# Attention with a soft mixture of experts: two heads at once on the row halves of TensorE

## The chip, the cores and the metric

The kernel runs on one NeuronCore of a Trainium2 chip. Its engines run side by side, each with its own queue, in the order in which the kernel issues the work: TensorE (PE; the loading of its weights is shown as PEld), VectorE (DVE), ScalarE (ACT), GpSimd (POOL) and SyncE (SP), which issues the DMAs here. The metric is the device time of one execution in microseconds (us); lower is better.

## The reference

For 8 batches of 8 heads, 576 positions and 64 dimensions per head, causal in blocks of 64:

```python
scores = 1/sqrt(D) * q @ k.T
scores = where(block_i >= block_j, scores, -1e9)       # blocks of 64 positions
attn = softmax(scores);  x = attn @ v                  # -> x: (8*576, 512)
logits = x @ phi                                       # (4608, 32): 8 experts x 4 slots
d = softmax over all 4608 rows of logits;  slot_input = d.T @ x
slot_out[e] = relu(slot_input[e] @ w1[e]) @ w2[e]      # 8 experts, 512 -> 1024 -> 512
out = softmax over slots of logits @ slot_out
```

All is float32. The weights w1 and w2 are 32 MB, in 32 pieces of 1 MB.

## The kernel before

The work has two stages. The attention stage handles 64 heads, in 32 pairs. The expert stage follows, from line 641: it turns the accumulated slot inputs into hidden rows (up, line 777), into slot outputs (down, line 804) and into the output (emit, line 739). The change leaves it as it is, except for one buffer count.

A head's 576 query rows are cut into tiles of 128 rows, called blocks 4, 3, 2, 1, from the end of the sequence, and a last 64 rows, block 0, which the two heads of a pair fill up to 128 together. Block t needs 128t + 64 columns of keys, so 576, 448, 320, 192 and 64. The upper 64 rows of a block are one step later in the sequence than the lower 64, so the lower ones have their last 64 columns masked (line 293, a matmul that adds -1e30; line 302 for block 0).

Scores (qk, lines 278 to 302). A float32 product is made out of rounded float32 (fp32r) matmuls over all 128 rows of the array: ACT rounds q (qh, line 204), POOL subtracts (ql, line 246), POOL scales k into the upper or lower 64 rows of ks (line 258), and DVE writes what the rounding lost into the other 64 rows (line 266). The two terms of k lie above each other in the 128 rows, q stands there twice, and two matmuls, with qh and with ql, add up a block of scores. Blocks 4 and 3 have two PSUM banks of their own (s43), blocks 2 and 1 share one (s21), block 0 takes one of three that rotate.

Softmax: DVE takes the negative row maximum (rowmax, line 310), ACT the exponential with the row sum (expo, line 316, followed by a read of the accumulator), DVE the reciprocal (zinv, lines 329 and 330), and DVE (block 3) or POOL (the others) multiplies (norm, lines 336 and 338).

Transposes (tr, lines 342 to 364; tr0, line 376). PE turns each 128 x 128 square of the probabilities in one matmul against an identity, with the probabilities as weights and the identity's 128 columns streaming; squares that are half masked are turned as 64 columns against a swapped identity (line 356), which puts two of them side by side. That is 14 per head and one per pair for block 0, in three banks A, B and C per head; ACT or DVE copies each bank out whole (evac).

Product with v (pv, line 390): the two heads of a pair write the two column halves of the array, in plain fp32, one key chunk of 128 after another. Block 0's queries share the first chunk's bank positions, and the last 64 columns have a product of their own. The transposed result xT is copied out (evac_x).

Mixture work, once per batch (four pairs): logits (part, lines 409 and 417), statistics, transposes of the logits and of xT (natural, xnat, line 497), and the accumulation of slot inputs (slots, line 510). It is spread over the next pairs.

What sets the order: every operation is put on a list with a due time (at); the times are in a table TM, in units of a head's period T, found beforehand by a planner. The list is sorted by time and issued in that order, and each engine and SP's queue keep it. EN says which engine does a copy. The weights are loaded in the attention stage as far as there is room (15 pieces stay resident in the arena, seven more come into areas as these become free), the rest in the expert stage.

Of the kernel before, what the change touches and what calls it, by code (L numbers as in the profile page):

```python
# [17 lines left out]
DM = H * D  # L18
# [9 lines left out]
COFF = {0: 0, 1: 576, 4: 1024, 2: 1088, 3: 1408}  # L28


NXN = 4
NXT = 6
NLK = 2
NV = 1
RINGX = "p4_0"
WARM = 11
RES = 15

PB = {4: 2, 3: 2, 2: 2, 1: 2}
XIN = (2,)  # L40
AREAS, LATE0 = {}, 0
for name, n in (
    ("lq0", S), *((f"lk{i}", S) for i in range(NLK)), ("lq1", S),
    *((f"p{t}_0", 128 * t + 64) for t in (4, 3, 2, 1) if PB[t] == 2 and f"p{t}_0" != RINGX), *((f"v{i}", 640) for i in range(NV - 1)),
    *((f"x{i}", S) for i in XIN), *((f"p{t}_{PB[t] - 1}", 128 * t + 64) for t in (4, 3, 2, 1)), ("pz", 128),
    ("pt0", 1600), ("pt1", 1600), *((f"v{i}", 640) for i in range(NV - 1, NV) if f"v{i}" != RINGX), ("phi", 512),
):
    AREAS[name] = (LATE0, LATE0 + n)
    LATE0 += n
NPIECE = 32  # L50
# [13 lines left out]
    "trC": 7.184, "evB": 10.029, "evA": 10.362, "evC": 7.809, "xb": 7.710, "xa": 2.149, "stats": (0, 12.875),  # L64
    "stats2": (0, 19.703), "nlt": (0, 13.687), "ndt": (0, 28.697), "disp": (0, 31.225), "xn0": (0, 3.906),
# [4 lines left out]
    "nltz": (0, 651.278), "ndtz": (0, 897.612), "dispz": (0, 2265.477), "xn0z": (0, 157.597),  # L70
    "en0z": (0, 396.824), "xn1z": (0, 749.778), "en1z": (0, 829.471), "xn2z": (0, 152.238),
    "en2z": (0, 478.997), "xn3z": (0, 651.280), "en3z": (0, 1377.835), "xn4z": (0, 1321.640),
    "en4z": (0, 2191.828), "saccz": (0, 2345.380), "loadq": 0.763, "loadk": 1.523, "loadv": -3.409,
# [7 lines left out]
}  # L81
EN = {
# [3 lines left out]
}  # L86
NB = B
# [4 lines left out]
def tile_attention_softmoe(  # L92
# [17 lines left out]
    swap = const.tile([128, 128], F32, name="swap")  # L110
    for i in range(2):
        nc.vector.tensor_copy(out=swap[:, 64 * i:64 * i + 64], in_=ident[:, 64 - 64 * i:128 - 64 * i])
# [10 lines left out]
    maskr = const.tile([128, 128], BF16, name="maskr")  # L123

    maskq = const.tile([128, 128], BF16, name="maskq")
    for x in (maskl, maskr, maskq):
        nc.vector.memset(x, 0.0)
    nc.vector.memset(maskq[0:1, 64:128], 1.0)
    for i in range(2):
        own, oth = slice(64 * i, 64 * i + 64), slice(64 - 64 * i, 128 - 64 * i)  # L130
        nc.vector.memset(maskl[32 * i:32 * i + 1, own], 1.0)
        nc.vector.memset(maskr[32 * i:32 * i + 1, oth], NEG)
# [32 lines left out]
    with ExitStack() as c1:  # L165
        xp = c1.enter_context(tc.tile_pool(name="xp", bufs=1, side="right"))
        sm = c1.enter_context(tc.tile_pool(name="sm", bufs=4, side="right"))
        ps = c1.enter_context(tc.tile_pool(name="ps", bufs=1, space=PSUM))
        ps_x = c1.enter_context(tc.tile_pool(name="ps_x", bufs=3, space=PSUM))

        s43 = ps.tile([128, 1024], F32, name="s43")
        s21 = ps.tile([128, 512], F32, name="s21")

# [744 lines left out]
```

## Time and profile before

| | us |
|---|---|
| median of three runs (491.8 to 493.0) | 491.83 |
| the profiled execution, whole | 491.81 |
| its span, first to last instruction | 490.0 |
| granted TensorE clock, mean of the span | 0.974 |

Stages of the profiled execution: scores from 6.4, the last scores at 397.7, the last product with v starts within the group from 405.8 to 409.3, experts from 423.7 to the end. A row of the profile gives line, engine, operation, what is written from what, shape, count, and then busy time in all and mean ns of one, and the idle time of the engine just before, with what ended it. In a timeline the columns are start, length, engine, line and operation, and how many like ones were merged.

### The profile page before, as it was taken

The page shows a single profiled execution, that of the slowest core. Times are in us where ns is not written, and L with a number is a line of the kernel's source. Part 1 is how long each engine was busy: PE and PEld are TensorE (multiplying, and loading weights), DVE is VectorE, ACT ScalarE, POOL GpSimd, SP SyncE. Part 2 cuts the span into 40 slices and gives each one's busy share as a digit, 9 for nine tenths or more (in the row PEclk, how much of TensorE's full clock was granted, in tenths as well). Part 3 has the DMA queues.
Part 4 walks back from the last instruction along what each step waited for, and adds up shares of the span by engine and source line. Part 5 has one row for each costly group of instructions (what it writes and reads, how often), then busy time and mean ns, then how long its engine had stood idle before and what let it go on. Part 6 is the DMA issues. An engine that isn't in the chain of part 4 may idle for free.

```text
span 490.0 us, 11349 instructions
## 1 busy us (share of the span) xinstructions
PE 466.9 (95%) x3815; PEld 310.3 (63%) x3815; DVE 396.5 (81%) x992; ACT 344.3 (70%) x1043; POOL 268.8 (55%) x372
## 2 busy tenths in 40 slices
PE   7899999999999999999999999999999999799990
PEld 3766676667666766676766676667666756344660
DVE  5999988988898889888988898989898973244571
ACT  3788788878787778777877787778777863012660
POOL 6776765666666666665666666656665730101100
PEclk9699999999999999999999999999999999799996
DMA  5735635455353544533654426354332119599698
GB/s 146 226 99 184 194 99 159 118 177 183 99 175 105 176 149 139 173 110 117 164 183 129 149 89 196 115 138 109 110 88 67 47 54 415 212 383 413 203 290 290
DMA packets 42697, 81.73 MB, mean 167 GB/s; under 512 B 8720, under 2 KB 26128, under 8 KB 38544
## 3 DMA queue, kind: packets, MB, share of 16 engines
q1 hardware_dynamic: 42640, 81.02, 52.1%
q8 instruction: 30, 0.49, 0.4%
q14 instruction: 27, 0.22, 0.2%
HBM read 71.57 MB, written 9.44 MB: 165 GB/s over the span
## 4 chain that ended last, share of the span: by engine, by line
PE 90%; DVE 3%; ACT 2%; DMA 1%; issue 1%; SPq 1%; POOL 0%; DVEq 0%; POOLq 0%; ACTq 0%
PE pv L390 23%; PE s L287 22%; PE pt_C L362 6%; PE pt_B L362 4%; PE pt_A L362 4%; PE xn L497 4%; PE pt_B L356 4%; PE hp L777 3%; PE so L804 3%; PE pt_A L356 3%; PE o L739 2%; PE lg L409 2%; PE s L293 2%; PE si L510 2%; PE lg L417 2%; PE s L301 1%
## 5 line engine op out<-in xcount | busy, mean ns | idle before, releaser
L316 ACT ACTIVATE arena<-s,stat 128x320 f32<-128x320 f32 (+4 forms) x256 | 135.7, 538 | 50.9 <-DVE stat L310 41.5
L338 POOL TENSOR_SCALAR arena<-arena,stat 128x320 f32<-128x320 f32 (+2 forms) x192 | 104.1, 554 | 95.5 <-DVE stat L329 88.1
L310 DVE TENSOR_REDUCE stat<-s 128x1 f32<-128x320 f32 (+4 forms) x288 | 136.1, 516 | 14.0 <-PE s L287 13.9
L287 PE MATMUL s<-ks,qh 128*128 128x320 f32 (+4 forms) x320 | 122.9, 384 | 1.6 <-ACT arena L316 1.6
L390 PE MATMUL pv<-arena 128*64 128x512 f32 (+5 forms) x768 | 117.1, 409 | 0.0
L246 POOL TENSOR_TENSOR ql<-arena,qh 128x576 fp32r<-128x576 f32 x64 | 91.5, 1429 | 32.5 <-ACT qh L204 29.9
L287 PE MATMUL s<-ks,ql 128*128 128x320 f32 (+4 forms) x320 | 101.3, 317 | 0.8 <-POOL ql L246 0.8
L287 PEld LDWEIGHTS s<-ks,qh 128*128 128x128 f32 (+1 forms) x320 | 60.2, 188 | 29.9 <-ACT arena L204 13.0
L266 DVE SCALAR_TENSOR_TENSOR ks<-arena,ks 64x576 fp32r<-64x576 f32 x64 | 75.1, 1174 | 4.9 <-POOL ks L258 3.0
L390 PEld LDWEIGHTS pv<-arena 128*64 128x64 f32 (+1 forms) x768 | 41.3, 134 | 51.0 <-issue 40.4
L287 PEld LDWEIGHTS s<-ks,ql 128*128 128x128 f32 (+1 forms) x320 | 58.8, 184 | 1.4 <-POOL ql L246 1.2
L316 ACT ACTIVATION_READ_ACCUMULATOR arena<-s,stat 128x1 f32 x256 | 52.5, 205 | 0.0
L258 POOL TENSOR_SCALAR ks<-arena 64x576 fp32r<-64x576 f32 x64 | 42.7, 667 | 12.4 <-PE s L287 9.0
L204 ACT CAST qh<-arena 128x576 fp32r<-128x576 f32 x64 | 43.4, 678 | 8.6 <-DMA arena<-in_q 5.0
L336 DVE TENSOR_SCALAR arena<-arena,stat 128x448 f32<-128x448 f32 x64 | 43.6, 682 | 0.0
L293 PE MATMUL s<-maskr,maskq 128*128 128x64 bf16 x192 | 39.4, 205 | 0.0
L204 ACT COPY arena<-pt_A 128x512 f32<-128x512 f32 x64 | 38.4, 600 | 0.5 <-PE pt_A L362 0.4
L204 ACT COPY arena<-pt_B 128x512 f32<-128x512 f32 x64 | 37.7, 590 | 0.4 <-PE pt_B L362 0.4
L362 PE MATMUL pt_C<-ident,arena 128*128 128x128 f32 x224 | 35.3, 275 | 0.0
L293 PEld LDWEIGHTS <-maskq 128*128 128x128 bf16 x192 | 18.6, 97 | 21.0 <-issue 14.2
L330 DVE RECIPROCAL stat<-stat 128x2 f32<-128x2 f32 (+1 forms) x160 | 26.5, 166 | 5.5
L362 PE MATMUL pt_A<-ident,arena 128*128 128x128 f32 x160 | 27.9, 273 | 0.0
(166 smaller groups left out, 776.7 us busy)
## 6 DMA issues: line engine op xcount, KB each, us to landing
arena<-in_w SPq DMA_DIRECT2D x30, 1024.0 KB, 7.7
arena<-in_q SPq DMA_DIRECT2D x128, 144.0 KB, 3.0
arena<-in_k SPq DMA_DIRECT2D x32, 288.0 KB, 3.4
arena<-in_v SPq DMA_DIRECT2D x32, 256.0 KB, 3.2
out<-arena SPq DMA_DIRECT2D x16, 512.0 KB, 4.1
wr<-in_w SPq DMA_DIRECT2D x2, 1024.0 KB, 8.4
arena<-in_v SPq DMA_DIRECT2D x32, 32.0 KB, 2.7
out<-arena SPq DMA_DIRECT2D x16, 64.0 KB, 3.2
```

Of the source, the lines that this page charges most:

```text
L204: nc.scalar.copy(out=out, in_=in_)
L246: (nc.gpsimd if EN["ql"] == "g" else nc.vector).tensor_tensor(out=qld, in0=src, in1=qhd.bitcast(F32), op=ALU.subtract)
L258: nc.gpsimd.tensor_scalar(out=ks[own, sl], in0=src, scalar1=SCALE, scalar2=0.0, op0=ALU.mult, op1=ALU.add)
L266: nc.vector.scalar_tensor_tensor(out=ks[oth, sl], in0=src, scalar=SCALE, in1=ks[own, sl].bitcast(F32), op0=ALU.mult, op1=ALU.subtract,)
L287: nc.tensor.matmul(pss[t][0:n, lo:hi], lhsT=qq[:, o:o + n], rhs=ks[:, k0 + lo:k0 + hi], start=(i == 0), stop=(i == 1 and not mask),)
L293: nc.tensor.matmul(pss[t][:, hi - 64:hi], lhsT=maskq, rhs=maskr[:, 64:128], start=False, stop=True)
L310: nc.vector.tensor_reduce(out=st[:, 0, u:u + 1], in_=src, axis=AX.X, op=ALU.max, negate=True)
L316: nc.scalar.activation(out=pr, in_=src, func=AF.Exp, bias=st[:, 0, u:u + 1], accum_out=st[:, 1, u:u + 1])
L336: nc.vector.tensor_scalar(out=pr, in0=pr, scalar1=st[:, 2, u:u + 1], scalar2=None, op0=ALU.mult)
L338: nc.gpsimd.tensor_scalar(out=pr, in0=pr, scalar1=st[:, 2, u:u + 1], scalar2=0.0, op0=ALU.mult, op1=ALU.add)
L362: nc.tensor.transpose(out=ptb[bank][:, o:o + 128], in_=probs[h, t][:, 128 * c:128 * c + 128], identity=ident)
L390: nc.tensor.matmul(xps[m, lo][64 * j:64 * j + 64, 0:n], lhsT=v_of(m)[0:k, j, c, :], rhs=pt_of(2 * m + j)[0:k, o:o + n], start=(c == cs[0]) ...
```

## The change

Both heads of a pair are worked on together, and the array is used in row halves: head 0 in rows 0 to 63, head 1 in rows 64 to 127.

- Scores are plain fp32: q comes as one load of 640 columns for the pair (block 0's rows padded with zeros), k is scaled for both heads in one POOL instruction, and there is no qh, ql or second term of k. qk has three steps per pair: U1 (block 4, first 512 columns), U2 (block 3 and the 64-column tail of block 4), U3 (blocks 2 and 1). In each the two heads' matmuls alternate. One masking matmul per head closes U2 and U3. Block 0 is one plain matmul over the whole array.
- Each head has two PSUM banks (sc): blocks 4 and 3 fill them, and blocks 2 and 1 go into the first of them after block 4 has been read. Two banks (ptb) take all transposes, and two (xbk) everything else, each at a bank given in the table.
- Transposes are of 64 rows by 128 columns against a 64 x 64 identity, upper half into one bank, lower half into the other. A head has two groups: group 1 is key chunks 0 and 1, group 2 chunks 2 to 4; tr10 is group 1 of head 0, tr21 group 2 of head 1. There are 24 per head and two for block 0. Probabilities have 64 more columns, kept at zero. Each group is copied out by two strided copies (e for the upper, o for the lower half).
- The order of all engines is new (TM, in units of a pair's period). PE's order over one period is U2, tr21, tr11, block 0, U3, the 64-column product, the five other products with v, tr20, U1, tr10; the groups tr21 and tr11 and the products belong to the pair before. The normalisation of block 3 moves from DVE to POOL; copies of the transposes and of xn, and the small ones of the logits, are shared out anew.
- One more weight piece stays resident (16). POOL zeroes the padding at the start: ten small areas and four of 64 x 512.

```diff
+        xbk = [ps.tile([128, 512], F32, name=f"x{i}") for i in range(2)]
+        sc = [ps.tile([128, 1024], F32, name=f"sc{j}") for j in range(2)]
+        ptb = [ps.tile([128, 512], F32, name=f"pt_{x}") for x in "eo"]
+        pss = {
+            (j, t): sc[j][:, lo:hi] for j in range(2) for t, (lo, hi) in
+            {4: (0, 576), 3: (576, 1024), 2: (0, 320), 1: (320, 512)}.items()
+        }
...
+        for j in range(2):
+            for t in range(1, 5):
+                nc.gpsimd.memset(area(f"p{t}_{j}")[:, 128 * t + 64:128 * t + 128], 0.0)
...
+        for x in xns:
+            nc.gpsimd.memset(x[64:128, :], 0.0)
...
-        def split_q(h, part):
-        def split_k(h, part):
...
+        def scale_k(m):
+            nc.gpsimd.tensor_scalar(
+                out=area(f"ks{m % NQB}"), in0=area("kr"), scalar1=SCALE, scalar2=0.0, op0=ALU.mult, op1=ALU.add
+            )
...
+        def qk(m, u):
+            q, k = area(f"q{m % NQB}"), area(f"ks{m % NQB}")
+
+            parts = {
+                1: [(4, 0, 512, 0)], 2: [(3, 0, 448, 576), (4, 512, 64, 512)], 3: [(2, 0, 320, 0), (1, 0, 192, 320)],
+            }[u]
+            for i, (t, k0, n, o) in enumerate(parts):
+                for j in range(2):
+                    r = slice(64 * j, 64 * j + 64)
+                    nc.tensor.matmul(
+                        sc[j][:, o:o + n], lhsT=q[r, 128 * (4 - t):128 * (4 - t) + 128], rhs=k[r, k0:k0 + n],
+                        start=(i == 0), stop=(u == 1),
+                    )
+            if u > 1:
+                lo, hi = {2: (512, 960), 3: (256, 448)}[u]
+                for j in range(2):
+                    r = slice(64 * j, 64 * j + 64)
+                    o = sc[j][:, lo:(hi + 64)].rearrange("p (n s) -> p n s", s=64)[:, ::(hi - lo) // 64, :]
+                    nc.tensor.matmul(
+                        o, lhsT=maskl[r], rhs=maskr[r].unsqueeze(1).broadcast_to([64, 2, 64]), start=False, stop=True
+                    )
...
+        GROUPS = {
+            1: ([(c, t) for c in (0, 1) for t in (4, 3, 2, 1)], [(0, 4), (0, 3), (0, 2), (0, 1), (1, 4), (1, 3), (1, 2)]),
+            2: ([(2, 4), (2, 3), (2, 2), (3, 4), (3, 3), (4, 4)], [(2, 4), (2, 3), (3, 4)]),
+        }
...
+        def tr(h, g):
+            cols = [list(x) for x in GROUPS[g]]
+            if (h % 2, g) in ((0, 2), (1, 1)):
+                cols[h % 2].append((0, 0))
+            for n in range(len(cols[0])):
+                for i in range(2):
+                    if n < len(cols[i]):
+                        c, t = cols[i][n]
+                        r = slice(64 * i, 64 * i + 64)
+                        nc.tensor.transpose(
+                            out=ptb[i][:, 64 * n:64 * n + 64], in_=probs[h - h % 2 if t == 0 else h, t][r, 128 * c:128 * c + 128],
+                            identity=ident[r, r],
+                        )
...
+        def pv(m, c):
+            if (m, c < 0) not in xps:
+                xps[m, c < 0] = xbank("pb" if c >= 0 else "pa")
...
-            p0, bm = mo[b, "ndt"], mo[b, "bm"]
-            dn = xp.tile([128, NQ, NS], F32, tag="dn", name=f"dn_{b}")
...
```

More of the change, by code (lines that the diff above doesn't have):

```diff
@@ L49 @@
     LATE0 += n
+XIN = (2,)
+RING, RING0 = {}, 0
+for name, n in (
+    *((f"q{i}", 640) for i in range(NQB)), ("kr", S), *((f"ks{i}", S) for i in range(NQB)), ("p3_0", 512), ("p3_1", 512),
+):
+    RING[name] = (RING0, RING0 + n)
+    RING0 += n
 NPIECE = 32
@@ L122, in tile_attention_softmoe @@
     maskl = const.tile([128, 128], BF16, name="maskl")
-    maskr = const.tile([128, 128], BF16, name="maskr")
-    maskq = const.tile([128, 128], BF16, name="maskq")
-    for x in (maskl, maskr, maskq):
+    maskr = const.tile([128, 64], BF16, name="maskr")
+    for x in (maskl, maskr):
         nc.vector.memset(x, 0.0)
[L128 to L132, printed above, removed]
+    for j in range(2):
+        nc.vector.memset(maskl[64 * j:64 * j + 1, 64:128], 1.0)
+        nc.vector.memset(maskr[64 * j:64 * j + 1, :], NEG)
     c_all = const.tile([128, B, NQ, NS], F32, name="c_all")
@@ L271, in warm @@
         def warm(i):
             if i == 0:
[L273 removed]
+                xps["w"] = xbank("pb")
             nc.tensor.matmul(
[L275 removed]
+                xps["w"], lhsT=maskl, rhs=maskr.unsqueeze(1).broadcast_to([128, 8, 64]), start=True, stop=True
             )
[L278 to L293 removed]
@@ L606, in tile_attention_softmoe @@
-        for m in range(NH // 2 - NXT, NH // 2):
+        tl = (NM - 1) * T
+        end_q = tl + max(TM[k] for k in ("U1", "U2", "U3", "S0")) + 0.01
+        end_r = max(end_q, tl + max(TM[f"tr{g}{j}"] for g in (1, 2) for j in range(2)) + 0.01)
+        end_v = tl + max(TM[k] for k in ("pva", *(f"pv{c}" for c in range(NQ)))) + 0.01
+        ends = {f"p{t}_{j}": tl + max(TM[f"tr{g}{j}"] for g in (1, 2)) + 0.01 for t in (4, 2, 1) for j in range(2)}
+        ends["pz"] = tl + max(TM["tr20"], TM["tr11"]) + 0.01
@@ L613, in swap_ring @@
+        ends["phi"] = tb + max(TM[f"prt{i}z"] for i in range(NQ)) + 0.01
         def swap_ring():
```

371 lines of the change are left out of this document (133 added, 238 removed), and 39 rows, old and new, of tables (EN, TM).

## The prediction

> **What bounds the kernel now.** I read the page first, for busy shares and the chain; then the first and last instance of something that happens once per pair of heads, for the period; then the engines between those two moments; last the timeline of TensorE inside one pair, because its busy time alone cannot say whether it is at its limit.
>
> ```profile
> span 490.0 us, 11349 instructions
> PE 466.9 (95%) x3815; PEld 310.3 (63%) x3815; DVE 396.5 (81%) x992; ACT 344.3 (70%) x1043; POOL 268.8 (55%) x372
> PE 90%; DVE 3%; ACT 2%; DMA 1%; issue 1%; SPq 1%; POOL 0%; DVEq 0%; POOLq 0%; ACTq 0%
> ```
>
> PE is nine tenths of the chain that ended last. The next two lines are the one full-size transpose that each pair has (line 376, with its first and last start), and the busy time of PE, PEld, DVE, ACT and POOL between those starts.
>
> ```profile
> L376 PE MATMUL t<-ident,arena x32: 272/273/329, 21.0 to 403.0; 128*128 128x128 f32 x32
> 21.00:403.00 382.00, 381.06 (x3091) 260.93 (x3089) 344.14 (x849) 306.08 (x949) 247.61 (x339) 1.00 0.45 132
> ```
>
> The 31 periods take 382.0 us, 12.32 us each, at a granted clock of 1.00. PE is idle for 0.9 us of them all; per pair DVE has 11.1 us of work, ACT 9.9, POOL 8.0. So in the attention stage a microsecond saved on PE per pair is worth 31 us, until something else comes late. From 423.67 on the experts run, which the change leaves alone but for one more resident weight piece:
>
> ```profile
> 423.67 6.90 PE L777 MATMUL hp<-arena,siT 128*32 128x512 f32 x48 [0.49 <-DVE siT L660]
> ```
>
> **The scores on PE.** A matmul's row lasts longer than the array is taken, so I go by the distance between starts.
>
> ```profile
> 205.24 0.22 PE L301 MATMUL s<-ks,qh 128*128 128x128 f32 x1
> 205.45 0.22 PE L287 MATMUL s<-ks,qh 128*64 128x64 f32 x1
> ...
> 209.34 0.47 PE L287 MATMUL s<-ks,qh 128*128 128x448 f32 x1
> 209.86 0.20 PE L293 MATMUL s<-maskr,maskq 128*128 128x64 bf16 x1
> 209.90 0.47 PE L287 MATMUL s<-ks,qh 128*128 128x512 f32 x1
> ...
> 210.54 0.34 PE L390 MATMUL pv<-arena 128*64 128x64 f32 x4
> 210.80 0.24 PE L287 MATMUL s<-ks,qh 128*64 128x64 f32 x1
> 211.04 0.49 PE L390 MATMUL pv<-arena 128*64 128x320 f32 x2
> ...
> 214.15 0.39 PE L287 MATMUL s<-ks,qh 128*128 128x320 f32 x1
> 214.89 0.28 PE L356 MATMUL pt_A<-swap,ringx 128*64 128x128 f32 x1
> ```
>
> One head costs 1.20 us for the blocks of 448 and 512 columns (209.34 to 210.54), 0.74 for those of 320 and 192 (214.15 to 214.89) and 0.24 for the tail of 64 (210.80 to 211.04); the pair shares 0.21 for block 0 (205.24 to 205.45). That is 2 x 2.18 + 0.21 = 4.57 us per pair.
>
> The new scores are plain fp32. The kernel already has plain fp32 on two halves of the array: line 390, each head on its own 64 columns. Each plain matmul shows there as two passes.
>
> ```profile
> 208.33 0.65 PE L390 MATMUL pv<-arena 128*64 128x512 f32 x2
> 208.81 0.60 PE L390 MATMUL pv<-arena 128*64 128x512 f32 x2
> ```
>
> Two heads' first passes start together, and their second passes together 0.48 us later: 0.05 for the first weight load, 0.43 for 512 columns of both. So two passes of 512 columns cost 0.86 us for both heads. If row halves do as column halves do, the 1536 columns of a pair (512 + 64, 448, 320, 192) cost 1536/512 x 0.86 = 2.6 us. Weight loads of 128 fp32 columns come to it, 0.11 each by the first two rows here:
>
> ```profile
> 209.34 0.19 PEld L287 LDWEIGHTS s<-ks,qh 128*128 128x128 f32 x1 [0.81 <-ACT arena L204]
> 209.45 0.19 PEld L287 LDWEIGHTS s<-ks,ql 128*128 128x128 f32 x1
> 138.83 0.14 PEld L497 LDWEIGHTS xn<-ident,xT 128*128 128x128 f32 x1 [0.28 <-issue]
> 138.89 0.14 PEld L497 LDWEIGHTS xn<-ident,xT 128*128 128x128 f32 x1
> ```
>
> Most hide behind long passes; I count four exposed (0.4), the two masks 0.15, and block 0 on the whole array 0.3. Sum 3.5 us, a saving of 1.1. The trace has no two row halves in flight at once, so the bounds are no overlap (2.6 us more: a loss of 1.5) and full overlap; I take the latter, because the column halves of the same plain fp32 show it (two rows of 0.64 within 0.65).
>
> **The transposes.** Now there are 14 per head and one per pair, 29, each streaming 128 columns:
>
> ```profile
> 213.46 0.27 PE L362 MATMUL pt_B<-ident,ringx 128*128 128x128 f32 x1
> 213.57 0.27 PE L362 MATMUL pt_B<-ident,arena 128*128 128x128 f32 x1
> 213.68 0.27 PE L362 MATMUL pt_B<-ident,ringx 128*128 128x128 f32 x1
> ```
>
> 0.11 us each, 3.2 per pair. After the change there are 50 of 64 rows (24 per head, two for block 0), alternating between the row halves: 29 slots, the odd half leaving some empty. Each streams 64 columns, half of 0.11, against a load of 128 columns that took 0.06 (138.83 to 138.89, transposes after a pause). A slot is then 0.057 us with both halves at work, 1.65 per pair: 1.5 saved. Bounds: all 50 one after another, 2.85, still 0.3 saved; a slot no shorter than now, nothing saved.
>
> Line 390's products keep their columns (the last one's rows are filled up with zeros). PE's work falls from 12.3 to 12.3 - 1.1 - 1.5 = 9.7 us per pair.
>
> **The other engines.** Per pair the change takes away and moves this:
>
> ```profile
> L266 DVE SCALAR_TENSOR_TENSOR ks<-arena,ks 64x576 fp32r<-64x576 f32 x64 | 75.1, 1174 | 4.9 <-POOL ks L258 3.0
> L246 POOL TENSOR_TENSOR ql<-arena,qh 128x576 fp32r<-128x576 f32 x64 | 91.5, 1429 | 32.5 <-ACT qh L204 29.9
> L204 ACT CAST qh<-arena 128x576 fp32r<-128x576 f32 x64 | 43.4, 678 | 8.6 <-DMA arena<-in_q 5.0 <-ACT arena L316 3.5
> L336 DVE TENSOR_SCALAR arena<-arena,stat 128x448 f32<-128x448 f32 x64 | 43.6, 682 | 0.0
> L338 POOL TENSOR_SCALAR arena<-arena,stat 128x576 f32<-128x576 f32 x32 | 24.0, 751 | 0.0
> L206 DVE COPY arena<-pt_C 128x512 f32<-128x512 f32 x32 | 22.1, 689 | 6.8 <-PE pt_C L362 6.3
> L204 ACT COPY arena<-pt_A 128x512 f32<-128x512 f32 x64 | 38.4, 600 | 0.5 <-PE pt_A L362 0.4
> ```
>
> DVE loses two of L266 (2.35), two of L336 (1.36) and the pt_C copy (0.69), and gets copies of 448, 512 and 256 columns (1.64 at 0.69 per 512) and small copies from ACT: about 8.6. ACT loses two casts (1.36) and about 580 columns of copying (0.7): 7.8. POOL loses two of L246 (2.86) and one of its two k scalings, and gets two normalisations of 448 columns (at most 0.75 each): under 7. None is the bound by its load.
>
> **Which wait ends last then.** PE could do 9.7, but the order now has loops that the old one avoided: the scores of blocks 2 and 1 (U3) overwrite the bank of block 4, so U3 waits for both block-4 exponentials, and the next pair's U1 waits for the exponentials of blocks 2 and 1; two banks take all transposes, and each of the four groups waits until both were copied out. Durations:
>
> ```profile
> L310 DVE TENSOR_REDUCE stat<-s 128x1 f32<-128x576 f32 x64 | 47.7, 746 | 7.1 <-PE s L287 7.1
> L310 DVE TENSOR_REDUCE stat<-s 128x1 f32<-128x320 f32 x64 | 30.3, 473 | 0.0
> L316 ACT ACTIVATE arena<-s,stat 128x576 f32<-128x576 f32 x32 | 23.7, 742 | 15.7 <-DVE stat L310 15.7
> L316 ACT ACTIVATE arena<-s,stat 128x448 f32<-128x448 f32 x64 | 40.9, 638 | 0.0
> L316 ACT ACTIVATE arena<-s,stat 128x320 f32<-128x320 f32 x64 | 34.1, 534 | 34.8 <-DVE stat L310 25.3 <-POOL ringx L338 9.2
> L316 ACT ACTIVATE arena<-s,stat 128x192 f32<-128x192 f32 x64 | 26.8, 419 | 0.0
> L316 ACT ACTIVATION_READ_ACCUMULATOR arena<-s,stat 128x1 f32 x256 | 52.5, 205 | 0.0
> ```
>
> Each of U1 (block 4's first 512 columns), U2 (block 3 and block 4's tail) and U3 (blocks 2 and 1) is 512 columns, 0.86 us, with load and mask 0.9, 1.1 and 1.2. I count from X, when U2 leaves PE. PE does the previous pair's tr21 (six slots, 0.35). On ACT its two copies stand ahead of the exponentials: 0.55 to 1.3 (384 and 256 columns at 0.6 per 512). The block-4 maxima (0.75 each on DVE) are ready by then. Two exponentials of 0.74, with the last accumulator read (0.2), end at 3.0: U3 starts at 3.1. Until then PE has tr11, block 0 and, in most pairs, a slice of the mixture work, so this wait is covered; without that slice it costs about 1 us. U3 (1.2) ends at 4.3; 0.2 later DVE does the maximum of block 2 (0.47), two reciprocal steps (0.3) and a maximum below 0.47: 5.6. Then ACT does blocks 1, 2, 2, 3, 1: 0.42 + 0.53 + 0.53 + 0.64 + 0.42 + five reads of about 0.1 net = 3.0, and U1 may start at 8.8. PE meanwhile does the pv group (1600 columns at 0.86 per 512, with loads 2.8, and one wait of 0.3 for the copy out of the bank that block 0, the 64-column product and the big one share) and tr20 (0.4): 7.8. It waits 1.0. U1 (0.9), tr10 (0.5) and U2 (1.1) end at 11.3 = the next X.
>
> That is with whole row durations; they overlap by about 0.1 per instruction on DVE and ACT, and seven to eight stand in this chain, which gives 10.5. The mixture's copies and statistics on DVE and ACT, once per four pairs, push it up again. I take 11.0, nearer to the chain than to the 9.7 of PE alone: 31 x (12.32 - 11.0) = 41 us.
>
> **Start and end.** POOL gets zeroings ahead of the first k scaling, four of half this size and ten smaller ones:
>
> ```profile
> 0.87 0.53 POOL L139 MEMSET acc<- 128x512 f32 x1
> ```
>
> at most 0.53 each for the four and 0.2 for the rest, 3 to 4 us. U1 starts at about 7.2 rather than 6.4, the price of work that nothing covers. The first pair's tr20 then comes at 7.2 + 2 + 7.8 = 17 where the old once-per-pair transpose stands at 21.0: 4 us gained. After the last pair's transposes the same tail follows, with POOL's nine normalisations in a row, 1 us more. SP's queue loses four q loads per pair for one, and v's load has its single buffer free from the end of pv to the next, some 7 us; no cost taken. Sum against the profiled execution (490.0 span, 491.81 in all; the median of the runs is 491.83): 491.8 - 41 - 3 = 448 us.
>
> **The rivals.** (1) The order's loops bind harder: mixture copies land in the middle of the two loops and each of the group waits adds 0.2. Period 11.6 to 12.2: 467 to 485. For it: two banks only for everything that had three. Against: ACT and DVE have 3 us of slack. Chance 0.13. (2) The loops hide wholly and PE's 9.7 to 10.3 rules: 408 to 426; chance 0.08. (3) Slower: row halves do not overlap. 2.6 us of scores and 21 more transpose slots (1.2) come to PE, 13.5, with about 0.6 of waits 14.1: 491.8 + 31 x 1.8 - 3 = 544. It decides once over a third of the 3.8 us is lost. For it: no row here shows row halves together. Against: the column halves. Chance 0.08. (4) Weights of a half load only while that half is idle: a slot becomes 0.06 + 0.05 = 0.11, so the transposes gain nothing (1.55 back), and ten score passes show 0.11 each (0.7 more): PE 11.95, with waits 12.8, so 491.8 + 31 x 0.5 - 3 = 504. Against it: the rows at 213.46 to 213.68 are 0.11 apart though each has a load of 0.06 before it in the same rows. Chance 0.06.
>
> The Trainium skill ("TensorE: Matmul & The Clock Gate", Part 3, The mechanism) says for packed tiles that weight loads overlap running matmuls only where the row group differs, which is rival 4; by that rule the time would be the 504. This trace does not bear it out for the full array. The same part gives 3.07 times for four row tiles of 32, which speaks against rival 3; no run here shows it yet.
>
> (5) No change within 0.3% (about what a measurement of this kernel can tell): 0.03.
>
> **How the numbers follow.** The main case, period 10.3 to 11.6 or 426 to 467, has 0.62; with (1) and (2) faster has 0.83; slower 0.14 from (3) and (4). From 422 to 484 the range holds the main case, nearly all of (1) and part of (2), about 0.8.
>
> **What would show it.** Right: plain score matmuls of the two heads starting within some ns of each other, second passes 0.43 us after the first for 512 columns; transpose pairs 0.06 apart; 31 periods of about 11.0; PE idle for about a tenth, its waits ended by ACT's exponentials (U1, U3) and by the copies of the transpose banks. Wrong: matmuls of the halves one after the other, slots of 0.11, or DVE's or POOL's work ending PE's waits.

## The result, and the profile after

| | before | after |
|---|---|---|
| median, us | 491.81 (4 runs) | 537.69 (4 runs, 534.75 to 540.2) |
| ratio, with its interval | | 1.093 [1.086, 1.099] |
| profiled execution / span, us | 491.81 / 490.0 | 540.2 / 538.4 |
| granted clock, mean of the span | 0.974 | 0.900 |

The forecast of 448 (422 to 484, slower 0.14) was wrong, in sign too. The profiled executions of e1 and e8 below were slow ones of their kernels (e1: 504.5 us against 495.12 to 497.98), so their rows are read mainly for order and waits.

The page of the profile after the change: busy time, granted clock in 40 slices, and the chain that ended last.

```profile
PE 449.8 (84%) x4391; PEld 269.5 (50%) x4391; DVE 323.6 (60%) x963; ACT 285.3 (53%) x875; POOL 187.1 (35%) x355
...
PEclk9577887999898889888997899988998989989996
...
PE 74%; ACT 14%; DVE 5%; issue 3%; POOL 2%; ACTq 0%; DVEq 0%; POOLq 0%
```

Before, PE had 95% of the span and 90% of the chain. Now it has 84% and 74%; ACT has come into the chain with 14%, and the clock row shows 7s and 8s all along. PE is busy for less time, and for a smaller share; the waiting and the clock took more than was saved.

Block 0 (line 276) stands once per pair and gives the period. The window from its first to its last start: length, then busy time of PE, PEld, DVE, ACT and POOL (with counts), the granted clock, and last the DMA share and GB/s.

```profile
8.94:437.50 428.56, 365.72 (x3629) 224.16 (x3629) 275.32 (x823) 251.90 (x793) 170.29 (x310) 0.90 0.32 106
```

31 periods take 428.56 us, 13.82 each, against 12.32 before: 31 x 1.50 = 46.6 of the 48.4 us by which the span grew. So what lies before the first of these starts and after the last hardly matters; the pairs do. To see it without the clock, here is block 0 at four pairs in a row with the clock at 1.00 throughout (each pair has two such matmuls; the row counts from the first of the first pair to the first of the fourth):

```profile
L276 PE MATMUL x<-rings x7: 222/275/323, 99.1 to 137.6; 128*128 128x64 f32 x7
```

Three periods take 38.5 us, 12.83 each. The same three places of the four-pair cycle before:

```profile
L301 PE MATMUL s<-ks,qh x4: 221/222/306, 81.0 to 117.1; 128*128 128x128 f32 x4
```

36.1 for three, 12.03. At full clock a pair at these places is thus 0.80 us longer. Where the whole growth lies can be read from block 0's first start in every pair. The first row is before, the others are after: the first four pairs of each, and then two pairs at the same place of the cycle.

```profile
9.55:55.65 46.10, 42.61 (x292) 30.03 (x291) 41.85 (x100) 36.17 (x110) 33.04 (x44) 0.89 0.52 155
...
8.87:69.15 60.28, 45.38 (x404) 28.12 (x400) 31.67 (x93) 31.69 (x97) 22.64 (x41) 0.75 0.31 102
69.15:82.94 13.79, 12.11 (x124) 7.63 (x120) 8.17 (x25) 7.65 (x26) 5.50 (x10) 0.88 0.42 144
124.58:137.60 13.02, 11.34 (x125) 7.41 (x121) 8.07 (x25) 7.55 (x26) 5.49 (x10) 1.00 0.42 152
```

Taken from block 0 in both kernels, the 31 periods grew by 46.1 us. The first four pairs take 14 of these, at a clock of 0.75, the other 27 periods 32. The longer loop at the three places makes 17 of these (1.0, 0.1 and 1.4 us at each, as the periods at a clock of 1.00 show). The other 15 lie in periods with a lowered clock: 6 at the three places, and 9 in the seven at the fourth place, none of which ran at 1.00. The last two rows show what the clock does: PE stands 1.68 us in both periods, and the one at 0.88 is 0.8 us longer.

Where PE waits, by groups (busy in all, mean ns, then idle before it and what ended that):

```profile
L260 PE MATMUL sc<-rings 64*128 64x512 f32 (+4 forms) x640 | 128.8, 469 | 51.9 <-ACT rings L294 50.5 <-POOL rings L239 1.4
```

PE stood before score matmuls for 50.5 us, 1.6 per pair, until an exponential on ACT that writes into "rings". By the names these are the exponentials of block 3, not of block 4, which write into "arena". The timeline shows it (start, length, engine, line); the first three rows are transposes of an earlier pair, the others belong to one pair:

```profile
240.82 0.22 PE L333 MATMUL pt_e<-ident,rings 64*128 64x64 f32 x1
240.82 0.22 PE L333 MATMUL pt_o<-ident,rings 64*128 64x64 f32 x1
240.88 0.22 PE L333 MATMUL pt_e<-ident,arena 64*128 64x64 f32 x1
...
327.62 0.26 PE L333 MATMUL pt_o<-ident,arena 64*128 64x64 f32 x1
...
329.70 0.74 ACT L294 ACTIVATE arena<-sc,stat 128x576 f32<-128x576 f32 x1
330.34 0.19 ACT L294 ACTIVATION_READ_ACCUMULATOR arena<-sc,stat 128x1 f32 x1
330.44 0.58 ACT L206 COPY arena<-pt_o 128x512 f32<-128x512 f32 x1
330.90 0.33 ACT L294 ACTIVATE arena<-x,stat 128x64 f32<-128x64 f32 x1
331.20 0.64 ACT L294 ACTIVATE rings<-sc,stat 128x448 f32<-128x448 f32 x1
331.72 0.22 ACT L294 ACTIVATION_READ_ACCUMULATOR rings<-sc,stat 128x1 f32 x1
331.99 1.14 PE L260 MATMUL sc<-rings 64*128 64x320 f32 x8 [1.46 <-ACT rings L294]
...
333.11 0.34 PE L358 MATMUL x<-arena 128*64 128x64 f32 x4
```

The transposes that follow U2 start at 327.62: that is X. The second of the block-4 exponentials is read out at 330.5, X + 2.9, as forecast (3.0). But U3 starts only at 331.99, X + 4.4. Between them stand on ACT the lower copy of tr11 (evo11, 0.46 to the next start), block 0's exponential (ex00, 0.30) and block 3's of head 0 (ex30, 0.74 to the end of its read). In the list they stand at 1.342, 1.864 and 1.867, U3 at 2.001. U3 writes columns 0 to 512 of the scores tile, ex30 reads 576 to 1024: no column in common, not even a bank.

The other part of the loss, by windows:

```profile
229.00:236.50 7.50, 5.76 (x91) 4.12 (x88) 4.64 (x13) 4.54 (x13) 1.16 (x3) 1.00 0.11 33
236.50:239.90 3.40, 3.40 (x12) 1.01 (x10) 2.14 (x9) 2.40 (x9) 2.58 (x5) 0.51 0.98 352
240.00:250.20 10.20, 8.46 (x114) 6.38 (x110) 6.52 (x19) 5.52 (x16) 2.91 (x5) 1.00 0.22 75
```

In the first window PE stands 1.7 of 7.5 us; in the 3.4 us after it the granted clock is 0.51, although PE is then busy throughout; then 1.00 again. The experiments had to tell the two losses apart, and each from what the row halves do themselves.

Steps are called below as in the list: rm, ex and nm are the row maximum, exponential and normalisation, followed by block and head (ex30: block 3, head 0); xa is the copy of the 64-column product, which stands before the five other products with v.

### The profile page after: what moved, and what is told of

Its sections match the earlier page's. It is cut to its first block, busy times and chain, and to the rows that moved or that the text cites. A ratio compares the mean times of both kernels' runs of the same rounds, so it can differ in the third digit from the quotient of the medians.

```text
span 538.4 us, 11941 instructions
## 1 busy us (share of the span) xinstructions
PE 449.8 (84%) x4391; PEld 269.5 (50%) x4391; DVE 323.6 (60%) x963; ACT 285.3 (53%) x875; POOL 187.1 (35%) x355
## 4 chain that ended last, share of the span: by engine, by line
PE 74%; ACT 14%; DVE 5%; issue 3%; POOL 2%; ACTq 0%; DVEq 0%; POOLq 0%
PE x L358 24%; PE sc L260 22%; PE pt_e L333 6%; ACT arena L294 5%; PE pt_o L333 4%; PE x L466 4%; ACT rings L294 4%; ACT arena L206 3%; PE hp L736 3%; PE so L763 3%; DVE stat L289 3%; PE o L698 2%; PE x L377 1%; PE x L385 1%; ACT xT L206 1%
## 5 line engine op out<-in xcount | busy, mean ns | idle before, releaser
L289 DVE TENSOR_REDUCE stat<-sc 128x1 f32<-128x576 f32 (+3 forms) x256 | 135.9, 549 | 111.7 <-PE sc L269 80.5
L260 PE MATMUL sc<-rings 64*128 64x512 f32 (+4 forms) x640 | 128.8, 469 | 51.9 <-ACT rings L294 50.5
L358 PE MATMUL x<-arena 128*64 128x64 f32 (+4 forms) x768 | 130.4, 480 | 9.0 <-ACT xT L206 7.8
L313 POOL TENSOR_SCALAR arena<-arena,stat 128x576 f32<-128x576 f32 (+3 forms) x224 | 116.8, 532 | 47.7 <-DVE stat L304 42.4
L294 ACT ACTIVATE arena<-sc,stat 128x576 f32<-128x576 f32 (+2 forms) x192 | 108.0, 564 | 43.7 <-DVE stat L289 35.4
L260 PEld LDWEIGHTS sc<-rings 64*128 64x128 f32 x640 | 66.1, 196 | 81.5 <-ACT rings L294 55.8
L358 PEld LDWEIGHTS x<-arena 128*64 128x64 f32 x768 | 56.9, 159 | 80.6 <-issue 59.4
L333 PE MATMUL pt_e<-ident,arena 64*128 64x64 f32 x672 | 86.7, 231 | 6.9 <-ACT arena L206 3.6
L333 PEld LDWEIGHTS pt_e<-ident,arena 64*128 64x128 f32 x672 | 68.9, 140 | 31.0 <-ACT arena L206 22.0
L333 PE MATMUL pt_o<-ident,arena 64*128 64x64 f32 x480 | 68.9, 236 | 0.0
```

The costliest lines, as they stand in the source:

```text
L260: nc.tensor.matmul(sc[j][:, o:o + n], lhsT=q[r, 128 * (4 - t):128 * (4 - t) + 128], rhs=k[r, k0:k0 + n], start=(i == 0), stop=(u == 1),)
L289: nc.vector.tensor_reduce(out=st[:, 0, u:u + 1], in_=scores(h, t), axis=AX.X, op=ALU.max, negate=True)
L294: nc.scalar.activation(out=pr[:, 0:128 * t + 64], in_=scores(h, t), func=AF.Exp, bias=st[:, 0, u:u + 1], accum_out=st[:, 1, u:u + 1],)
L313: nc.gpsimd.tensor_scalar(out=pr, in0=pr, scalar1=st[:, 2, u:u + 1], scalar2=0.0, op0=ALU.mult, op1=ALU.add)
L333: nc.tensor.transpose(out=ptb[i][:, 64 * n:64 * n + 64], in_=probs[h - h % 2 if t == 0 else h, t][r, 128 * c:128 * c + 128], identity=iden ...
L358: nc.tensor.matmul(xps[m, c < 0][64 * j:64 * j + 64, 0:n], lhsT=vs[:, j, max(c, 0), :], rhs=arena[:, lo:lo + n], start=(c <= 0), stop=(c < ...
```

## The experiments

My theory (A): U3 waits for ex30 because the program that turns the list into waits holds the two-bank scores tile for one thing, so that each access waits for the earlier listed ones of other engines; the idle time that results halves the clock in stretches. Rival B: the use of row halves lowers the clock by itself, and the waits are a consequence. Rival C: the halves do not really overlap.

**e1: U3 earlier in the list** (still behind both block-4 exponentials; PE's own order changes only once in four pairs, where U3 goes ahead of a small step of the mixture work).

```diff
-"U3": 2.001   (behind ex00 1.864 and ex30 1.867)
+"U3": 1.86
```

> Only the due time of U3 moves, from 2.001 to 1.86, so that it stands before block 0's and block 3's exponentials of head 0 in the list instead of after them. Theory A (order: U3 waits for block 3's exponential only because that is ahead of it in the list, and the half clock follows from the idle time): PE's idle time before U3 falls from 1.5 us per pair to under 0.5, the period from 13.8 to 11.2 to 11.8 us, the granted clock is 0.97 or more from 48 us on, and the time is 455 to 475 us. Rival B (work on row halves keeps the clock low by itself): the idle time falls, the clock stays at about 0.93, period 12 to 12.5, 480 to 500 us. Rival C (U3 waits for something the list does not set): nothing changes, 538 us.

Measured: 497.82 us (495.12 to 504.5), ratio to before 1.010 [1.006, 1.014]: 40 us less than the change, but above the time that A gave and inside the one that B gave. Groups, three pairs at full clock, timeline and windows:

```profile
L260 PE MATMUL sc<-rings 64*128 64x512 f32 (+4 forms) x640 | 133.7, 458 | 10.9 <-DVE stat L289 7.3 <-ACT arena L206 1.7 <-POOL rings L239 1.0
L289 DVE TENSOR_REDUCE stat<-sc 128x1 f32<-128x576 f32 (+3 forms) x256 | 135.8, 549 | 81.5 <-ACT rings L294 61.8 <-PE sc L269 17.4 <-ACT arena L294 2.2
```

```profile
L276 PE MATMUL x<-rings x7: 222/275/323, 90.7 to 127.1; 128*128 128x64 f32 x7
```

```profile
245.09 1.54 PE L260 MATMUL sc<-rings 64*128 64x512 f32 x3
246.47 0.59 PE L260 MATMUL sc<-rings 64*128 64x512 f32 x1
...
337.41 0.60 DVE L289 TENSOR_REDUCE stat<-sc 128x1 f32<-128x448 f32 x1
337.74 0.58 ACT L206 COPY arena<-pt_o 128x512 f32<-128x512 f32 x1
338.07 0.84 PEld L260 LDWEIGHTS sc<-rings 64*128 64x128 f32 x8 [0.23 <-DVE stat L289]
...
339.29 0.63 ACT L294 ACTIVATE rings<-sc,stat 128x448 f32<-128x448 f32 x1 [0.61 <-PE sc L269]
340.05 0.49 DVE L289 TENSOR_REDUCE stat<-sc 128x1 f32<-128x320 f32 x1 [1.21 <-ACT rings L294]
```

```profile
8.00:60.00 52.00, 42.38 (x324) 25.74 (x322) 28.16 (x87) 28.58 (x90) 20.29 (x37) 0.70 0.35 113
60.00:250.00 190.00, 176.36 (x1860) 110.19 (x1860) 137.34 (x410) 124.41 (x392) 85.24 (x155) 1.00 0.39 126
```

The wait of 50.5 us is gone, and three periods take 36.4, 12.13 each. Time and period lie where B had put them; it is the clock that decides. It is 1.00 from 60 to 250 us with the same use of row halves, so B falls.

What U3 waits for now shows what the list does. It starts at 338.07, when the maximum of block 3 (337.41 to 338.01), a read of the other bank, is done. The copy evo11, which also stands ahead of U3 in the list but has nothing to do with the scores tile, runs on to 338.32. So U3 waits for the earlier listed accesses of its own tile, whichever bank they touch, and not for all that is listed before it.

The waits also turned round with the list: ex30, now behind U3, starts when U3's masks on PE are done (339.29), and the maximum of block 2, behind ex30, starts when that is read out (340.05), though the two only read, and different banks. DVE stands 61.8 us there. U1's two heads, which can start together, are 0.9 us apart or more (245.09, the last pass at 246.47), head 1's waiting for its late block-1 exponential. I took these waits for the reason that the period fell to 12.1 and not to the expected 11.2 to 11.8; e6 and e9 test it.

**e2: fillers in the changed kernel.** The fillers are matmuls whose results change nothing. tr11 and block 0's product are issued twice.

> The waits stay, but PE does the last group of transposes (tr11) and block 0's product twice, 0.8 us per pair more work that lies in the idle time before U3. Theory A: the wait of U3 ends when it did, PE's idle time before it falls to about 0.7 us, the half-clock stretches mostly go, the period comes to 12.7 to 13.0 and the time to 503 to 515 us, faster with more work. Rival B (transposes of row halves do not keep the clock up): clock 0.90 to 0.93 as before, time 538 us or more.

Measured: 539.72 us, ratio 1.098 [1.094, 1.102]. The mean clock rose from 0.900 to 0.944, the time did not fall to the expected 503 to 515. The fillers stood in the very loop: they delay block 0's product, so its maximum, ex00, ex30 and U3. Three periods at the same places of the cycle, with no lowered clock, now take 40.4, 13.5 each against 12.83:

```profile
L277 PE MATMUL x<-rings x13: 222/275/323, 150.0 to 190.4; 128*128 128x64 f32 x13
```

What the clock gave, the longer loop took. The experiment shows that PE's idleness moves the clock, but it was badly placed to show the worth of that.

**e3: U2 and U3 with all of head 0's matmuls ahead of head 1's.**

```diff
-            for i, (t, k0, n, o) in enumerate(parts):
-                for j in range(2):
+            for j in range(2):
+                for i, (t, k0, n, o) in enumerate(parts):
```

> In U2 and U3 all matmuls of head 0 are issued before those of head 1, instead of in turns (U1 has one per head and stays). If the halves overlap only where neighbours in the queue lie in different halves: U2 and U3 take up to 0.9 us more each, both on the path, period +1.5 to 1.8, 585 to 595 us. If PE's queue looks far enough ahead to overlap them anyway: no change, 538 us. I expect the former, perhaps in part.

Measured: 538.66 us, no difference from the change; U3's eight matmuls still take 1.14 us as a group. I had expected a loss: the order of issue within such a group does not decide whether the halves overlap.

**e4: all upper 64-row transposes of a group ahead of the lower ones.**

> In each group all transposes of the upper half are issued before those of the lower. If neighbours must lie in different halves to overlap: 50 slots of 0.06 us instead of 29, 1.3 us of PE per pair more, half of it on the path, 550 to 575 us (a little less if the clock gains from a busier PE). If the order does not matter: 538 us.

Measured: 546.45 us, ratio 1.111: 9 us more than the change, less than expected, at a mean clock of 0.88 to 0.89 against 0.90 to 0.91. The timeline shows why it is less: only the first few of the upper half run alone, the later ones of each half run beside the other half's.

```profile
104.59 0.22 PE L333 MATMUL pt_e<-ident,arena 64*128 64x64 f32 x1
104.65 0.22 PE L333 MATMUL pt_e<-ident,rings 64*128 64x64 f32 x1
```

These two are of one half, with nothing on the other, and each has a weight load of its own; they start 0.06 us apart.

**e5: e1 with 30 unread matmuls at PE's idle places in the first three pairs.**

```diff
+FILL = ((0, "U3", 8), (0, "tr20", 12), (1, "U3", 2), (1, "pv0", 2), (1, "tr20", 2), (2, "U3", 2), (2, "tr20", 2))
+            nc.tensor.matmul(
+                xbk[1], lhsT=maskl, rhs=maskr.unsqueeze(1).broadcast_to([128, 8, 64]), start=True, stop=True
+            )
```

> e1's order (U3 ahead of ex00 and ex30), and 30 more matmuls on the mask constants, 128x512 in bf16, into an unused bank, put where PE stands idle in the first three pairs (8 before the first U3, 12 before the first tr20, 2 each at seven places... in all 30); nothing reads them. In e1 the granted clock was 0.70 from 8 to 60 us and 1.00 from 60 to 408, with no difference in the work. If the idle time of the first pairs (2.0 us before the first U3, 3.1 before the first tr20) halves the clock (my theory), the clock of that stretch rises above 0.9, its four pairs go from 56.6 to about 50 us, and the kernel takes 488 to 492 us. If the use of row halves or something else of the first pairs lowers it, the clock stays at 0.7 and the time at 496 to 500.

Measured: 501.34 us, ratio 1.019 [1.015, 1.022], not the expected 488 to 492. The stretch did as the theory has it, in part:

```profile
8.00:60.00 52.00, 47.35 (x408) 27.78 (x405) 30.35 (x92) 29.78 (x93) 22.75 (x41) 0.90 0.37 122
```

The clock rose from 0.70 in e1's profile to 0.90. The first four pairs take 52.8 us (first block 0 at 8.9, fifth at 61.7) against 56.6, so 3.8 were gained there, not 7. The fourth of them has no fillers and is the same in both, 14.1 us at 0.76. The whole was no faster, and the mean clock of its executions (0.957 to 0.970) no higher than in e1. In the 65 us after the last pairs the clock was 0.82, in the like stretch of e1's profile 0.84; that this ate the gain is not shown.

**e6: the list of e1 with accesses to the scores tiles set apart, and xa on DVE.** After U3 DVE takes head 1's maxima while ACT takes ex30, and each exponential stands behind the maxima that need not wait for it.

```diff
-"rm31": 3.92,  "rm21": 3.242, "rm11": 4.956, "ex31": 4.712, "ex20": 3.983, "ex21": 4.588, "ex11": 5.362
+"rm31": 2.8,   "rm21": 2.45,  "rm11": 2.5,   "ex31": 3.9,   "ex20": 3.0,   "ex21": 2.6,   "ex11": 3.5
-"zh0": 2.704, "zh1": 6.4,  "zl1": 6.068, "xa": "a"
+"zh0": 2.55,  "zh1": 4.55, "zl1": 4.5,   "xa": "v"
```

> e1's order, and the accesses to the two scores tiles listed so that none stands behind another engine's access that it doesn't need: after U3 DVE takes head 1's blocks 2 and 1 (rm21, rm11) while ACT takes ex30, then rm20, rm10, rm31; the exponentials follow as ex30, ex21, ex20, ex10, ex11, ex31; the 64-column copy xa goes from ACT to DVE. If each access to a scores tile waits for all earlier listed accesses of that tile by other engines, of either bank (my theory), the 1.8 us per pair that DVE stands before its row maxima in e1 fall under 0.6, ex11 ends 0.6 to 1.0 earlier after U3, U1's two heads start together again (they stand 0.85 us apart in e1), the period of 12.3 us comes to 11.3 to 11.7 and the time to 466 to 480. If only overlapping columns count, or if PE's own work sets the period, it stays at 494 to 500.

Measured: 483.0 us, ratio 0.981 [0.978, 0.984]: faster than before. The time is 3 us above the range, the mechanism as expected:

```profile
L289 DVE TENSOR_REDUCE stat<-sc 128x1 f32<-128x448 f32 (+3 forms) x256 | 133.0, 549 | 39.3 <-PE sc L269 37.0 <-ACT arena L294 2.3
```

```profile
L276 PE MATMUL x<-rings x7: 222/275/323, 81.8 to 115.9; 128*128 128x64 f32 x7
```

DVE's 61.8 us behind exponentials have gone; what is left is the honest wait for the scores themselves. Three periods take 34.1, 11.37 each. The fourth of the cycle, with the mixture work, is longer.

**e7: e5 and e6 together.**

> Both edits of e5 and e6 in one kernel. If the two causes are separate, their gains add: 458 to 472 us, a granted clock above 0.98 over the whole, and a period of 11.3 to 11.7 from the first pairs on. If the clock falls again because the shorter period leaves other idle time, it stays near 480.

Measured: 481.1 us, ratio 0.977 [0.974, 0.980], and not the expected 458 to 472; the intervals of e6 and e7 overlap, so the fillers' worth is not told from nothing here. e6 had little to gain at the start: its clock from 8 to 60 us was 0.93 already.

**e8, e9: the two parts of e6 alone**, xa on DVE, and the new order with xa left on ACT.

> e1's order with the 64-column copy xa on DVE instead of ACT, alone of what e6 changes. In e1 PE stands 0.47 us per pair before pv0 for that copy, in e6 still 0.41. If the new list order of the accesses to the scores tiles made e6's gain (my theory), this stays at 494 to 500 us; if the copy made it, it comes to 481 to 487.

Measured: 506.79 us (500.08 to 508.49), ratio 1.021 [1.014, 1.028]. Nothing gained against e1; the two intervals just touch.

> e1's order and e6's order of the row maxima and exponentials, with the copy xa left on ACT. If the list order makes e6's gain: 481 to 489 us. If the copy does: 494 to 500.

Measured: 477.91 us, ratio 0.972 [0.969, 0.975], below the range and better than e6. So the order made the whole gain. Moving xa cost some 5 us: e6 is that much above e9, and e8 above e1.

```profile
223.26 0.69 PE L260 MATMUL sc<-rings 64*128 64x512 f32 x1
...
223.38 1.07 PE L260 MATMUL sc<-rings 64*128 64x512 f32 x3
224.22 0.23 PE L333 MATMUL pt_o<-ident,arena 64*128 64x64 f32 x1
...
224.66 0.64 PE L260 MATMUL sc<-rings 64*128 64x448 f32 x1
...
225.69 0.22 PE L269 MATMUL sc<-maskr,maskl 64*128 64x128 bf16 x1
```

```profile
8.00:64.00 56.00, 45.83 (x420) 29.47 (x420) 32.95 (x95) 32.50 (x101) 22.75 (x41) 0.79 0.33 114
64.00:250.00 186.00, 168.06 (x1883) 109.25 (x1879) 142.54 (x427) 127.74 (x406) 88.36 (x160) 1.00 0.41 137
```

U1's heads start 0.12 us apart, and U1 leaves PE after 0.96 us (223.26 to 224.22).

**e10: e6 with both heads' score and mask matmuls on array rows 0 to 63.**

```diff
-                    r = slice(64 * j, 64 * j + 64)
+                    r = slice(0, 64)
```

> e6 with the scores and mask matmuls of both heads on array rows 0 to 63, so that none can run beside another; it computes head 0's scores twice and head 1's not at all. If the passes of the two heads lie one over the other on row halves, as the prediction's term of 3.5 us per pair has it, the scores matmuls' 2.8 us of PE per pair grow by 2.2 to 2.8, and the time by 55 to 90 us, to 540 to 572. If row halves bring nothing, it stays near 483.

Measured: 593.37 us, 110 more than e6, more than expected.

```profile
228.91 1.07 PE L260 MATMUL sc<-rings 64*128 64x512 f32 x2
...
230.69 0.22 PE L333 MATMUL pt_e<-ident,arena 64*128 64x64 f32 x1
231.18 2.11 PE L260 MATMUL sc<-rings 64*128 64x448 f32 x8
233.13 0.22 PE L269 MATMUL sc<-maskr,maskl 64*128 64x128 bf16 x1
```

```profile
L276 PE MATMUL x<-rings x7: 222/275/323, 115.5 to 158.0; 128*128 128x64 f32 x7
```

U1 takes 1.78 us (228.91 to 230.69) instead of 0.96, U2 up to its masks 1.95 instead of 1.03 (224.66 to 225.69 in e9). Three periods take 42.5, 14.17 each, 2.80 more than e6: 31 x 2.80 = 87 us, within what was expected; the other 24 or so lie in the first pairs and at the fourth place, where the clock is lower than in e6 (mean of the span 0.914 against 0.966). C falls: row halves in plain fp32 do overlap, and for the scores and masks they are worth 2.8 us a pair at full clock.

**e11: e6's order in the changed kernel, U3 left where it was, xa on ACT** (e9 with "U3" at 2.001).

> The changed kernel's list with e6's order of row maxima and exponentials alone: U3 stays behind ex30 in the list, as in the changed kernel, and the copy xa on ACT. If U3's wait for ex30 is the larger cause and halves the clock as well (my theory), PE still stands some 1.4 us per pair before U3, the clock stays near 0.9, and the time falls by 10 to 25 us only, to 513 to 528. If the order behind U3 were the whole of it, it would come to 481 to 490.

Measured: 548.93 us, ratio 1.115 [1.112, 1.119]: slower than the change, where I had expected 10 to 25 us less.

```profile
L260 PE MATMUL sc<-rings 64*128 64x512 f32 (+4 forms) x640 | 123.6, 485 | 51.6 <-ACT rings L294 50.2 <-POOL rings L239 1.4
```

```profile
L276 PE MATMUL x<-rings x7: 222/275/323, 153.9 to 191.8; 128*128 128x64 f32 x7
```

PE stands before U3 as before (50.2 us). At full clock the better order does help, 37.9 for three periods, 12.63 each instead of 12.83; but the mean clock is 0.871 instead of 0.900. At full clock PE stands 2.1 to 2.3 us per period at these places, where it was 1.7 to 1.8. That this lowers the clock fits the other runs, but nothing here shows it apart.

**e12: e9 with the fillers of e5.**

> The list of e9 and the 30 unread matmuls of e5 in the idle places of the first three pairs. In e9 the granted clock is 0.79 from 8 to 64 us and 1.00 from 64 to 400, and its first four pairs take 53.9 us, those of e7 (with the fill) 46.4. If PE's idle time in the first pairs halves the clock there (my theory), the stretch comes to a clock above 0.95 and the four pairs to 46 to 48 us; the time falls by up to 7, to 470 to 477 us, less what the clock of the stretch after the last pair takes back (in e7 3.5 us). If not, it stays at 477 to 481.

Measured: 475.98 us (475.5 to 478.25), ratio 0.969 [0.966, 0.971], the best time of the study, though its interval overlaps e9's.

```profile
8.00:64.00 56.00, 49.99 (x518) 30.59 (x516) 38.13 (x113) 37.07 (x116) 27.78 (x51) 1.00 0.47 145
```

The clock of the first 56 us is 1.00 instead of 0.79, and the first four pairs take 46.5 us instead of 53.9. Only 4.9 of these 7.4 are left in the span (473.8 against 478.7) and 2 in the medians. One later pair lost 1.1 us to a clock of 0.88, and after the last pairs the clock was lower this time (0.92 from 359 to 425 us; in e9 0.95 from 366 to 432).

The four kernels that have U3 early or late and the old or new order, all with xa on ACT:

| | old order | new order |
|---|---|---|
| U3 behind ex30 | 537.7 (the change) | 548.9 (e11) |
| U3 ahead of ex30 | 497.8 (e1) | 477.9 (e9) |

The early U3 is worth 40 us in the old order and 71 in the new. The new order gives its gain only once U3's wait is gone: it is worth 20 us with an early U3 and loses 11 with a late one.

## Why the prediction was wrong

**The scores and the transposes on PE: right.** The scores were put at 0.9, 1.1 and 1.2 us for U1, U2 and U3; the rows give 0.96 (e9), 1.15 (e9: 224.66, masks from 225.69, 0.06 each) and 1.12 (after: 331.99 to 333.11). The transposes of the halves start within 0.01 us of each other and 0.06 apart (240.82, 240.88), as forecast. So the rivals "row halves do not overlap" and "weights of a half load only while that half is idle" fall. The Trainium skill ("TensorE: Matmul & The Clock Gate", Part 3) has it in its list that a weight load overlaps running matmuls only on another row group, while its text also allows a background weight buffer; the slots of 0.06 us with a load before each are not what the first gives, 0.11, nor are the 0.06 us between transposes of one half in e4. The 544 us of the first of these rivals is near the measured time by accident.

The sum of PE's work, 9.7 us a pair, was not seen in any run. In e9, from 64 to 250 us at a clock of 1.00, PE's rows fill 10.6 of the 11.7 us of a period. A row of PE lasts longer than the array is taken, so this does not show the sum to be too low either; it stays open.

**The other engines: right.** DVE was put at about 8.6 us per pair, ACT at 7.8, POOL under 7; the window over 31 periods gives 8.9, 8.1 and 5.5.

**The step that failed: "U3 waits for both block-4 exponentials ... U3 starts at 3.1".** The trace gives the exponentials' end at X + 2.9 and U3 at X + 4.4. I read the wait off the data: which columns U3 overwrites. It is set by the list: U3 stands behind ex30, and ex30 behind a copy and another exponential on ACT. Moving U3 in the list alone (e1) took the wait away; moving it back (e11) brought it back. The order of the list decides which of the two waits, and in e1 U3 waits for the earlier listed access of its own tile while an earlier listed one of another tile still runs. So it is the program that makes the semaphores, not the chip, that ties the two banks of the tile together. That rule is inferred from the waits. The Trainium skill ("PSUM — Partial Sum Buffer", section "PSUM bank collisions raise a hardware error") asks that engines be kept apart by bank and quadrant; the waits here go beyond it, over two banks. The prediction's second loop, "the next pair's U1 waits for the exponentials of blocks 2 and 1", was right, but its sum had no such waits either: e1 shows 61.8 us of them on DVE.

**"So this wait is covered": wrong in consequence.** U3 starts 1.3 us later than the forecast's X + 3.1, and this was not covered: PE stands 1.46 us in the pair shown, although it has mixture work there too. By the prediction's own chain, 11.0 + 1.3 = 12.3, against 12.83 at the three places at full clock.

**A term that was missing: the clock.** The prediction took 1.00 throughout, as before had it from 21 to 403 us, with PE idle for 0.9 us in all. After the change PE stands 1.7 us or more in every period, and the clock fell to half in stretches of 3.4 us and more. That idle time can lower it is shown by fillers alone: with them the clock from 8 to 64 us went from 0.79 to 1.00 (e12 against e9). Of the 46 us that the periods grew, some 17 are the longer loop at full clock and 15 lie in later periods with a lowered clock; 14 lie in the first four, where longer waits and half clock come together and were not told apart.

**The start: right at first.** U1 was put at 7.2 and starts at 6.8, the first pair's tr20 at 17 and starts at 17.1. But the 3 us that the sum counted as gained there were not: the first four pairs took 14 us more than before.

**The rivals.** "The order's loops bind harder" had the right place and far too small a price (a period of 11.6 to 12.2; measured 12.83 at full clock and 13.82 over all). It had no case with U3's wait and no clock. With the list mended, the change gives 477.9 us, inside the forecast's range and at that rival's 467 to 485. What separates this from 448 is the period, 11.33 at three places (87.3 to 121.3 in e9) and 13.1 at the fourth, and the clock at the start.

```profile
L276 PE MATMUL x<-rings x7: 222/275/323, 87.3 to 121.3; 128*128 128x64 f32 x7
```

**What stays open.** How much idle time, and where, tips the clock: stands of the same length tipped it in some pairs and not in others. Idle time as the rows show it is not the whole account either: in e6 the second and third periods ran at 1.00 with 1.8 us of it in 11, in e10 at 0.70 with 1.0 in 17. Why the fillers' gain at the start is partly lost again after the last pair was not settled.

## What to carry to other kernels

Before costing a wait by the data it needs, look at what the scheduling program holds to be the same buffer, and what stands ahead of it in the list: one place in the list was worth 40 us here, and an unneeded wait turns round, rather than goes, if only one of its sides is moved. A change that takes work off the bounding engine can also take away what keeps its clock up; cost the new idle time twice, once as waiting and once as clock, and test an order only after the larger wait is gone.

## What the runs showed of the hardware

- The granted clock fell to half after PE had stood 1.7 us within 7.5 us of otherwise dense work (after: 0.51 from 236.5 to 239.9 us). The Trainium skill ("TensorE: Matmul & The Clock Gate", section "HAM oscillation") gives as the abstract rule no gaps of more than about 3.4 us; here half of that came before the fall. It did not always: with 1.68 us of idle time in each, one period of the change ran at 0.88 and another, at the same place of the cycle, at 1.00.
- Two 64-row halves in plain fp32 give the work of one: 1.78 us for four passes of 512 columns on the same rows (e10), 0.96 on both halves (e9), and the order of issue within a group of eight such matmuls made no difference (e3).
- Transposes of one 64-row half alone, each with its own weight load, start 0.06 us apart (e4, 104.59 and 104.65).
